# Grouping the small attention matmuls of three units into one TensorE step (attention followed by a gated MLP)

## The chip, the cores and the metric

The kernel runs on one core of a Trainium2 chip. The metric is the device time of one execution in microseconds (us). TensorE (PE) does the matrix products, PEld is its weight load, DVE is VectorE, ACT is ScalarE, POOL is GpSimd, and SP issues the DMAs. The engines run side by side and wait for each other through semaphores; each executes its own instructions strictly in program order.

## The reference

There are 4 batches, 8 heads, 768 tokens and 64 features per head. Attention has a local part (keys within 16 tokens) and a summary part (24 blocks of 32 tokens, whose key is the block's maximum and whose value is the block's mean).

```
k_sum = k.reshape(B, H, nb, block, D).max(axis=3)
v_sum = v.reshape(B, H, nb, block, D).mean(axis=3)
scores_l = scale * (q @ k^T), kept where |i - j| < 16
scores_s = scale * (q @ k_sum^T) + log(32)
a = softmax over both parts
x = a @ concat(v, v_sum)                     # 768 x 512 per batch
xk = mu_k * x + (1 - mu_k) * x_prev          # x_prev: one token earlier
xr = mu_r * x + (1 - mu_r) * x_prev
out = sigmoid(xr @ w_r) * (relu(xk @ w_k)**2 @ w_v)
```

All data is float32. The products of the second part are each done as three products of 32-bit "r" values (high times high, high times low, low times high).

## The kernel before, in words

Attention is cut into *units*: one unit is one batch, one pair of heads and one half of the tokens, so there are 8 units to a batch and 32 in all. A unit goes through these steps.

- Scores on PE (line 501): 12 products, each on a 64x64 part of the array, float32, which show as 24 instructions in the trace, into two PSUM tiles `sc`.
- Mask and row minimum on DVE (512), exponential and row sum on ACT (516), six of each; then the sum's epsilon on ACT (521) and its reciprocal `rc` on DVE (523).
- Normalisation of the six slices by `rc`, the *norms*: on POOL or DVE (528) or on ACT (533), whichever the planner expects to be done first.
- Two *turns* on PE (540): three transposes each, into the only PSUM tile `pt`, each copied to `pts` by ACT (544).
- Values on PE (562): 12 products, 24 instructions, into the only PSUM tile `av`, copied out to `x` by DVE (574) or ACT (576).

A value window holds 96 token rows and 24 rows of block means. For batch 0 the means come from small products (437, 457) and are spread by POOL or DVE (465). For batches 1 to 3, `load_set` loads the values of one head pair transposed into a staging tile `st` (448, SP), sums blocks on DVE (449), transposes the 24 sums on PE (452), scales them on ACT (471) and writes them into the windows by DMA (474). So this happens 12 times.

The second part of the work is *wide* on PE: every product uses 128 rows and 128 columns of the array. A gate step is 12 products of 512 columns (639 to 641); the first expert layer has steps of 12 products of 384 columns (671); the second has steps of 6 and 3 products of 512 columns (693, 719). There are two halves of 384 tokens per batch, each with a gate, eight first-layer and eight second-layer steps. Weights are loaded as 64-bit words and converted at the start (343 to 382) on ACT, POOL and DVE.

The order on each engine is made at build time by a list scheduler, `Plan.schedule`. It takes operations by a start time, a due time (worked backward from gates and experts) and the constants in `LENGTH`; `NUDGE` shifts the due times of named tags. One `op` on PE is one step: its products stay together. Attention of batch b+1 is planned in between the experts of batch b, so that PE takes attention steps between wide steps. Until the first gate is done, idle time that the plan foresees on PE is filled by products on a zero tile `still` (788).

Of the kernel before, what the change touches and what calls it, by code (L numbers as in the profile page):

```python
# [39 lines left out]
    score=865, transpose=370, vtrans=200, vpool=900, vsel=240, spread=560, spread_p=900, values=1000, values0=1750, mixe=1480, minus=200, diag=290, wminus=1250, wevac=520, none=0, gate=2790, gate_p=2100, e1=2110,  # L40
    e2a=1400, e2b=700, e2=700, e2h=350, resulth=340,
    kred=860, kred2=460, kmax=90, kcopy=225, vred=865, mask=203, rc=110, evac=470, mixd=530, sub=472, psub=480, khv=300,
    result=605, wsign=575, eps=110, wor=605, wsub=605, tiny=60, wsign_d=335,
    exp=378, pts=362, vm=165, mixa=512, cast=405, relu=375, square=413, sigmoid=494, wscale=562, wcast=510,
    norm=340, norm_d=165, norm_a=285, mixa_d=300, wscale_p=575, wcast_p=575, mixa_p=575, kcopy_p=400, evac_a=362,
# [11 lines left out]
APART = False  # L57
# [5 lines left out]
    e000=-16000, e001=-1500, e002=-500, e003=2000, e004=1500, e005=1500, e006=-11000, e007=12500, e010=7500,  # L63
    e012=2500, e014=-59000, e015=-2500, e016=-4000, e017=50000, e100=-12000, e101=-5500, e102=-52000,
    e103=-1500, e106=7000, e107=34000, e111=-1000, e112=-9500, e113=-2500, e114=-41500, e115=4500, e116=2000,
    e117=2500, e200=17500, e201=-35500, e202=1500, e203=15500, e204=49000, e205=57000, e206=60000, e207=59500,
    e210=1500, e211=-11500, e212=6500, e213=26500, e214=28000, e215=27000, e216=42000, e217=58000, e300=1500,
    e301=500, e302=-38500, e303=-4000, e304=13000, e305=14000, e306=12000, e307=58500, e310=-42500, e311=-25000,
    e313=2000, e314=2000, e316=17500, e317=50500, f000=60000, f001=1500, f002=14000, f003=4000, f004=-26000,
    f005=-31500, f006=3500, f007=-27000, f011=-3000, f014=-15500, f015=13500, f016=-11500, f017=-500,  # L70
    f100=-1500, f101=-6500, f102=19000, f104=5500, f105=-4000, f106=36000, f107=-22500, f111=-12000, f113=-6500,
    f115=-14500, f116=16000, f117=-2000, f201=-500, f202=2000, f203=23000, f204=-39000, f206=-22000,
    f207=-21000, f210=-13000, f211=10500, f212=1000, f213=20500, f214=-54500, f215=-56500, f217=1500,
    f300=-30000, f301=-19500, f302=-25000, f303=1000, f304=57000, f305=22500, f307=23000, f310=-4500,
    f311=-57500, f314=10500, f315=-17000, f316=500, gate00=8500, gate01=43000, gate10=5500, gate11=-16000,
    gate20=38500, gate21=59500, gate30=-4000, gate31=59500, mix000=-3000, mix001=-1500, mix010=-11000,
    mix011=500, mix101=-23500, mix111=7000, mix200=-500, mix201=-9500, mix210=16000, mix211=3500, mix300=-28000,
    mix301=-23500, mix310=-15000, mix311=26000, set00=1000, set01=13000, set02=-7500, set10=-11000, set11=-5500,
    set12=-500, set13=-9500, set20=1000, set21=-16000, set23=1500, set30=4000, set31=-17500, set32=-6500,
    set33=13500, unit000=1500, unit011=500, unit020=500, unit021=-1000, unit030=-2500, unit031=3000,  # L80
    unit100=-60000, unit101=-6000, unit110=-6000, unit111=-7500, unit120=-41000, unit130=500, unit131=7500,
    unit200=1000, unit201=-1500, unit210=-1000, unit211=6000, unit221=8500, unit300=1000, unit301=-42000,
    unit310=-500, unit311=1000, unit320=-13500, unit321=7000, unit330=-38500, unit331=-60000, wk1=8000,
    wk3=-5000, wk4=2000, wk5=-9500, wk6=-7000, wk7=-45000, wr0=500, wr1=-1000, wr2=-3000, wr3=2000, wv0=2000,
    wv1=6500, wv2=4500, wv3=-56500, wv4=-33500, wv5=500, wv7=-5500,
# [9 lines left out]
NORM = "DVE", "ACT"  # L95
# [161 lines left out]
def tile_kernel(ctx: ExitStack, tc: tile.TileContext, q, k, vT, v, mask, ident, pool, sel, mu, w_k, w_v, w_r, out):  # L257
# [4 lines left out]
    def tiles(name, n, shape, dtype=F32, pool=const):  # L262
# [5 lines left out]
        vs=tiles("vs", 1, [P, NS]), vm=tiles("vm", 4, [P, P]), sp=tiles("sp", 2, [P, P]),  # L268
# [120 lines left out]
    def windows(vw):  # L389
        return vw.t[0:NK, 0:S].rearrange("p (w d) -> p w d", d=P)  # L390

    def load_set(b, p):
# [17 lines left out]
        kg, ks, vm = buf("kg"), buf("ks"), buf("vm")  # L410
# [19 lines left out]
        if b == 0:  # L430
            tp = buf("mm")

            def means():
                for i in range(3):
                    for g in range(4):
                        w = 3 * g + i
                        nc.tensor.matmul(
                            tp.t[32 * g:32 * g + 32, 0:P], pool_sb[:, 4 - 2 * i:36 - 2 * i],
                            windows(vw[w // HW])[:, w % HW, :], start=(i == 0), stop=(i == 2))

            op("PE", "vpool", None, means, reads=[(x, y) for x in vw for y in "ab"] + [*POOLM], writes=[(tp, 0)])
        else:
            vt, vs, tp = buf("st"), buf("vs"), buf("pt")

            def tokens():
                return vt.t[:, 0:S].bitcast(F32)

            op("SP", "load", None, lambda: nc.sync.dma_start(out=tokens(), in_=vT[b - 1, p]), writes=[(vt, 0)], size=P * S * 4)
            op("DVE", "vred", None, lambda: nc.vector.tensor_reduce(
                out=vs.t, in_=tokens().rearrange("p (n c) -> p n c", c=BLOCK), op=ALU.add, axis=AX.X),  # L450
               reads=[(vt, 0)], writes=[(vs, 0)])
            op("PE", "vtrans", None, lambda: nc.tensor.transpose(
                out=tp.t[0:NS, 0:P], in_=vs.t, identity=ident_sb), reads=[(vs, 0), *IDENT], writes=[(tp, 0)])
        if b == 0:
            sp, t2 = buf("sp"), buf("mm")
# [5 lines left out]
            if APART:  # L461
                e["vm"] = vm
            for x in () if APART else vw:
# [6 lines left out]
        else:  # L470
            op("ACT", "vm", None, lambda: nc.scalar.activation(
                vm.t[0:NS], tp.t[0:NS, 0:P], AF.Copy, scale=1.0 / BLOCK), reads=[(tp, 0)], writes=[(vm, 0)])
            for x in vw:
                op("SP", "load", None, lambda x=x: nc.sync.dma_start(
                    out=windows(x)[QW:KB], in_=vm.t[0:NS].unsqueeze(1).broadcast_to([NS, HW, P])),
                   reads=[(vm, 0)], writes=[(x, "b")], size=NS * HW * 512)
        return e

    def unit(b, p, hf, e, due):

        plan.tag = f"unit{b}{p}{hf}"
        kt, qt, vw = e["kt"], buf("qt"), e["vw"][hf]
        o = hf * HW
        op("SP", "load", None, lambda: nc.sync.dma_start(out=qt.t, in_=q[b, p, :, hf * HT:(hf + 1) * HT]),
           writes=[(qt, 0)], size=P * HT * 4)
        sc = [buf("sc") for _ in range(2)]
        y = [buf("y") for _ in range(2)]
        mn = [buf("mn") for _ in range(2)]
        sm, rc = buf("sm"), buf("rc")
        pt = [buf("pt") for _ in range(2)]  # L490
        pts = [buf("pts") for _ in range(2)]
        av = buf("av")


        def scores():
            for i in range(NSL):
                for h in range(2):
                    for c in range(2):
                        n = 2 * i + c
                        hs, cs, w = slice(h * D, (h + 1) * D), slice(c * QW, (c + 1) * QW), o + n  # L500
                        nc.tensor.matmul(  # L501
                            sc[h].t[cs, i, 0:NK], qt.t[hs, n * QW:(n + 1) * QW], kt.t[hs, w * KB:w * KB + NK],
# [3 lines left out]
        op("PE", "score", due - 10000, scores, reads=[*e["kparts"], (kt, "s"), (qt, 0)],  # L506
           writes=[(sc[0], 0), (sc[1], 0)])
        for h in range(2):
            for i in range(NSL):
                slot = hf * NSL + i  # L510
                var = 0 if slot == 0 else (2 if slot == 2 * NSL - 1 else 1)
                op("DVE", "mask", None, lambda h=h, i=i, var=var: nc.vector.tensor_tensor_reduce(  # L512
                    out=y[h].t[:, i, :], in0=sc[h].t[:, i, 0:NK], in1=mask_sb[:, var, :], scale=-SCALE, scalar=3.0e38,
                    op0=ALU.add, op1=ALU.min, accum_out=mn[h].t[:, i:i + 1]),
                   reads=[(sc[h], 0), *MASK], writes=[(y[h], i), (mn[h], i)])
                op("ACT", "exp", None, lambda h=h, i=i: nc.scalar.activation(  # L516
                    y[h].t[:, i, :], y[h].t[:, i, :], AF.Exp, bias=mn[h].t[:, i:i + 1], scale=-1.0,
                    accum_out=sm.t[:, NSL * h + i:NSL * h + i + 1]),
                   reads=[(y[h], i), (mn[h], i)], writes=[(y[h], i), (sm, NSL * h + i)])

        op("ACT", "eps", None, lambda: nc.scalar.activation(sm.t, sm.t, AF.Copy, bias=1.0e-9),
# [360 lines left out]
```

## Time and profile before

| what | value |
|---|---|
| median of 3 runs | 458.22 us (457.29 to 458.62) |
| profiled execution | 457.95 us |
| its span, first to last instruction | 456.1 us |
| PE busy | 448.0 us (98%) |
| DVE busy | 298.5 us (65%) |
| ACT busy | 296.2 us (65%) |
| POOL busy | 25.2 us (6%) |
| DMA queue of the loads and stores | 33.4% of 16 engines |

The time is the profiled execution's own time; about 1.85 us of it lie outside the span. Busy time of PE is modelled from pipelined matmuls, so a busy PE may still hide short waits. In the chain of waits each piece is the time that a stretch of work adds to the end: end of the piece before it to its own end.

### The profile page before, as it was taken

The page shows a single profiled execution, that of the slowest core. Times are in us where ns is not written, and L with a number is a line of the kernel's source. Part 1 is how long each engine was busy: PE and PEld are TensorE (multiplying, and loading weights), DVE is VectorE, ACT ScalarE, POOL GpSimd, SP SyncE. Part 2 cuts the span into 40 slices and gives each one's busy share as a digit, 9 for nine tenths or more (in the row PEclk, how much of TensorE's full clock was granted, in tenths as well). Part 3 has the DMA queues.
Part 4 walks back from the last instruction along what each step waited for, and adds up shares of the span by engine and source line. Part 5 has one row for each costly group of instructions (what it writes and reads, how often), then busy time and mean ns, then how long its engine had stood idle before and what let it go on. Part 6 is the DMA issues. An engine that isn't in the chain of part 4 may idle for free.

```text
span 456.1 us, 9735 instructions
## 1 busy us (share of the span) xinstructions
PE 448.0 (98%) x3599; PEld 378.2 (83%) x3599; DVE 298.5 (65%) x1016; ACT 296.2 (65%) x879; POOL 25.2 (6%) x54
## 2 busy tenths in 40 slices
PE   9999999999999999999999999999999999999996
PEld 8766788788988898888978897888888889889985
DVE  5999999999773956647565547958552456243122
ACT  3898999889785837588576548857775546232210
POOL 0332310001000000000000000100000000000000
PEclk9999999999999999999999999999999999999999
DMA  8963558665100085252300058414300010001001
GB/s 306 401 238 128 204 196 279 235 205 191 32 15 15 1 268 226 47 170 82 126 15 9 6 189 311 100 49 138 133 17 13 1 46 24 0 2 68 2 0 69
DMA packets 27446, 51.96 MB, mean 114 GB/s; under 512 B 2951, under 2 KB 15111, under 8 KB 27399
## 3 DMA queue, kind: packets, MB, share of 16 engines
q1 hardware_dynamic: 27399, 51.35, 33.4%
q8 instruction: 28, 0.46, 0.4%
q14 instruction: 19, 0.16, 0.1%
HBM read 43.28 MB, written 6.29 MB: 109 GB/s over the span
## 4 chain that ended last, share of the span: by engine, by line
PE 78%; DVE 16%; DMA 2%; issue 1%; ACT 1%; SPq 1%; DVEq 0%
PE mm L671 27%; PE mm L693 24%; PE av L562 4%; PE mm L639 4%; PE mm L641 4%; PE mm L640 4%; PE pt L540 4%; PE sc L501 4%; PE mm L719 4%; DVE y L528 2%; DVE we L355 2%; DVE wc L359 2%; DVE y L512 2%; DMA qt<-in_q 1%; DVE we L351 1%
## 5 line engine op out<-in xcount | busy, mean ns | idle before, releaser
L671 PE MATMUL mm<-xs,wk_h 128*128 128x384 f32 x512 | 101.6, 340 | 0.0
L671 PEld LDWEIGHTS mm<-xs,wk_h 128*128 128x128 f32 x512 | 89.9, 188 | 4.5 <-issue 0.5
L516 ACT ACTIVATE y<-y,mn 128x120 f32<-128x120 f32 x192 | 73.8, 387 | 9.2 <-DVE mn L512 8.9
L676 ACT ACTIVATE r<-mm 128x384 f32<-128x384 f32 x64 | 30.7, 488 | 73.3 <-PE mm L671 56.7
L693 PE MATMUL mm<-wv_h,kh 128*128 128x512 f32 x168 | 69.0, 411 | 0.0
L693 PE MATMUL mm<-wv_l,kh 128*128 128x512 f32 x168 | 66.4, 395 | 0.0
L512 DVE CUSTOM_DVE_ANT_0 y<-sc,mask_sb 128x120 f32<-128x120 f32 x192 | 43.2, 276 | 20.9 <-PE sc L501 11.7
L671 PE MATMUL mm<-xs,wk_l 128*128 128x384 f32 x256 | 55.2, 337 | 0.0
L682 DVE TENSOR_TENSOR kl<-r,kh 128x384 fp32r<-128x384 f32 x64 | 35.2, 553 | 28.5 <-PE mm L693 27.6
L680 DVE CAST kh<-r 128x384 fp32r<-128x384 f32 x49 | 17.3, 358 | 55.3 <-ACT r L678 27.4
L693 PE MATMUL mm<-wv_h,kl 128*128 128x512 f32 x168 | 51.4, 414 | 0.0
L671 PEld LDWEIGHTS mm<-xs,wk_l 128*128 128x128 f32 x256 | 45.6, 188 | 0.0
L599 DVE TENSOR_TENSOR xs<-xa,xs 128x384 fp32r<-128x384 f32 x60 | 32.5, 548 | 18.7 <-ACT xs L597 18.6
L639 PE MATMUL mm<-wr_h,xs 128*128 128x512 f32 x96 | 38.7, 404 | 0.0
L641 PE MATMUL mm<-wr_h,xs 128*128 128x512 f32 x96 | 38.0, 396 | 0.0
L640 PE MATMUL mm<-wr_l,xs 128*128 128x512 f32 x96 | 37.9, 395 | 0.0
L693 PEld LDWEIGHTS mm<-wv_h,kh 128*128 128x128 f32 x168 | 31.6, 188 | 7.0 <-issue 0.8
L544 ACT COPY pts<-pt 120x384 f32<-120x384 f32 x64 | 30.3, 474 | 10.3 <-PE pt L540 8.0
L693 PEld LDWEIGHTS mm<-wv_l,kh 128*128 128x128 f32 x168 | 31.7, 188 | 5.9
L516 ACT ACTIVATION_READ_ACCUMULATOR y<-y,mn 128x1 f32 x192 | 36.3, 189 | 0.0
L594 DVE SCALAR_TENSOR_TENSOR xa<-vx,mu_sb,xa 128x384 f32<-128x384 f32 x60 | 35.8, 611 | 0.5 <-ACT xa L587 0.2
L540 PE MATMUL pt<-ident_sb,y 128*120 128x128 f32 x192 | 32.7, 278 | 1.5 <-ACT pts L544 1.2
(82 smaller groups left out, 694.3 us busy)
## 6 DMA issues: line engine op xcount, KB each, us to landing
vx<-in_v SPq DMA_DIRECT2D x32, 384.0 KB
kt<-in_k SPq DMA_DIRECT2D x15, 544.0 KB
qt<-in_q SPq DMA_DIRECT2D x32, 192.0 KB
out<-z SPq DMA_DIRECT2D x23, 256.0 KB
st<-in_vT SPq DMA_DIRECT2D x12, 384.0 KB
st<-in_w_k SPq DMA_DIRECT2D x8, 512.0 KB
st<-in_w_v SPq DMA_DIRECT2D x8, 512.0 KB
st<-in_w_r SPq DMA_DIRECT2D x4, 512.0 KB
```

What stands on the lines that cost most here:

```text
L512: op("DVE", "mask", None, lambda h=h, i=i, var=var: nc.vector.tensor_tensor_reduce(out=y[h].t[:, i, :], in0=sc[h].t[:, i, 0:NK], in1=mask_ ...
L516: op("ACT", "exp", None, lambda h=h, i=i: nc.scalar.activation(y[h].t[:, i, :], y[h].t[:, i, :], AF.Exp, bias=mn[h].t[:, i:i + 1], scale=-1.0,
L540: nc.tensor.transpose(out=pt[h].t[0:NK, i * P:(i + 1) * P], in_=y[h].t[:, i, :], identity=ident_sb)
L594: op("DVE", "mixd", None, lambda xt=xt, xa=xa, p=p: nc.vector.scalar_tensor_tensor(out=xa.t, in0=xt.t[:, 1 + lo:1 + lo + HT], scalar=mu_sb ...
L599: op("DVE", "sub", None, lambda xa=xa, xh=xh, xl=xl: nc.vector.tensor_tensor(out=xl.t, in0=xa.t, in1=xh.t.bitcast(F32), op=ALU.subtract), ...
L639: nc.tensor.matmul(ps[i].t, xh.t[:, ts], wr_h[:, p, :], start=(p == 0), stop=False)
L640: nc.tensor.matmul(ps[i].t, xh.t[:, ts], wr_l[:, p, :], start=False, stop=False)
L641: nc.tensor.matmul(ps[i].t, xl.t[:, ts], wr_h[:, p, :], start=False, stop=(p == NPAIR - 1))
L671: nc.tensor.matmul(ps.t[:, 0:HT], w[:, j, p, :], x[p][s].t, start=(n == 0), stop=(n == 11))
L676: op("ACT", "relu", None, lambda: nc.scalar.activation(r.t, ps.t[:, 0:HT], AF.Relu), reads=[(ps, 0)], writes=[(r, 0)])
L682: op("DVE", "sub", None, lambda: nc.vector.tensor_tensor(out=kl.t, in0=r.t, in1=kh.t.bitcast(F32), op=ALU.subtract), reads=[(r, 0), (kh, 0 ...
L693: nc.tensor.matmul(acc[t].t, a.t[:, t * P:(t + 1) * P], w[:, j, :], start=start, stop=stop)
```

## The change

- The unit becomes a class `Unit`, whose `scores`, `turn` and `values` return what they would emit. `group` puts several of them into one PE step.
- From batch 1 on, `chain(b)` walks the 8 units. Its step i holds, in this order, the scores of unit i, the values of unit i-2 and the first turn of unit i-1. The second turn of unit i-1 stays a step of its own. A batch has one step with scores alone, one with scores and a turn, six with all three, one with values and a turn, and one with values alone.
- `block_means(b)` loads the transposed values of all four head pairs, sums their blocks into one 128x96 tile, and turns it in one transpose, with one scaled copy. So there are 3 such transposes and copies instead of 12; loads, DVE sums and the DMAs into the windows remain.
- `NORM` loses DVE: norms go to POOL or ACT.
- Constants in `LENGTH` and the whole `NUDGE` table are other numbers. `APART`, which was off, goes.

```diff
-NORM = "DVE", "ACT"
+NORM = ('ACT',)
...
-        vs=tiles("vs", 1, [P, NS]), vm=tiles("vm", 4, [P, P]), sp=tiles("sp", 2, [P, P]),
+        vs=tiles("vs", 1, [P, NPAIR * NS]), vm=tiles("vm", 4, [P, P]), sp=tiles("sp", 2, [P, P]),
...
+    def block_means(b):
+        plan.tag = f"means{b}"
+        vs, tp, vm = buf("vs"), buf("pt"), buf("vm")
+        for p in range(NPAIR):
+            vt = buf("st")
...
+            op("SP", "load", None, lambda p=p, tokens=tokens: nc.sync.dma_start(out=tokens(), in_=vT[b - 1, p]),
+               writes=[(vt, 0)], size=P * S * 4)
+            op("DVE", "vred", None, lambda p=p, tokens=tokens: nc.vector.tensor_reduce(
+                out=vs.t[:, NS * p:NS * p + NS], in_=tokens().rearrange("p (n c) -> p n c", c=BLOCK), op=ALU.add, axis=AX.X),
+               reads=[(vt, 0)], writes=[(vs, p)])
+        op("PE", "vtrans", None, lambda: nc.tensor.transpose(
+            out=tp.t[0:NPAIR * NS, 0:P], in_=vs.t, identity=ident_sb),
+           reads=[(vs, p) for p in range(NPAIR)] + [*IDENT], writes=[(tp, 0)])
+        op("ACT", "vm", None, lambda: nc.scalar.activation(
+            vm.t[0:NPAIR * NS], tp.t[0:NPAIR * NS, 0:P], AF.Copy, scale=1.0 / BLOCK), reads=[(tp, 0)], writes=[(vm, 0)])
+        return vm
...
+    def group(name, due, *parts):
+        emits = [x for x, _, _ in parts]
+        op("PE", name, due, lambda: [x() for x in emits],
+           reads=[r for _, rs, _ in parts for r in rs], writes=[w for _, _, ws in parts for w in ws])
...
+    def chain(b):
+
+        means = block_means(b)
+        units, n = [], 2 * NPAIR
+        for i in range(n + 2):
...
+            if i < n:
+                parts.append(units[i].scores())
+                due.append(units[i].due - 10000)
+            if i >= 2:
+                parts.append(units[i - 2].values())
+                due.append(units[i - 2].due - 1000)
+            if 1 <= i <= n:
+                parts.append(units[i - 1].turn(0))
+                due.append(units[i - 1].due - 3500)
...
-            for p in range(NPAIR):
-                e = load_set(b + 1, p)
-                for h in range(2):
-                    unit(b + 1, p, h, e, gate_due(b + 1, 0) - 14000 - (7 - 2 * p - h) * UNITS)
+            chain(b + 1)
```

PE, in the middle of batch 1's attention, before: the end of one unit's values (`av`), the transpose of one head pair's block sums (`vs_82`), a wide step (`wv`), a turn (`pt<-ident_sb,y`) and another wide step.

```order
L562 MATMUL av_146<-pts_104,vx_73 64x64
L452 MATMUL pt_145<-ident_sb,vs_82 24x128
L693 MATMUL mm_147<-wv_h,kh_133 128x512
L693 MATMUL mm_147<-wv_l,kh_133 128x512
L693 MATMUL mm_148<-wv_h,kh_133 128x512
L693 MATMUL mm_148<-wv_l,kh_133 128x512
L693 MATMUL mm_150<-wv_h,kh_133 128x512
L693 MATMUL mm_150<-wv_l,kh_133 128x512
L540 MATMUL pt_145<-ident_sb,y_89 120x128 x3
L693 MATMUL mm_147<-wv_h,kl_135 128x512
L693 MATMUL mm_148<-wv_h,kl_135 128x512
L693 MATMUL mm_150<-wv_h,kl_135 128x512
```

PE, the first full chain step of batch 1, after: the end of its scores and the start of its values.

```order
L511 MATMUL sc_143<-kt_62,qt_66 64x120 x2
L511 MATMUL sc_144<-kt_62,qt_66 64x120 x2
L577 MATMUL av_146<-pts_103,vx_72 64x64
L577 MATMUL av_146<-pts_104,vx_72 64x64
...
L557 MATMUL pt_145<-ident_sb,y_91 120x128 x3
L703 MATMUL mm_150<-wr_h,xs_114 128x512
L704 MATMUL mm_150<-wr_l,xs_114 128x512
```

Scores (`sc`), all twelve products of the values (`av`) and a turn now stand without a wide product between them; the wide gate products (`wr`) follow the turn. In the old order wide products stood between the values and the turn.

DVE, during batch 0's attention, before: norms (`y<-y,rc`) of two units between the pieces of weight conversion (`we`, `wc`).

```order
L523 RECIPROCAL rc_102<-sm_99 128x6
L528 TENSOR_SCALAR y_89<-y_89,rc_102 128x120 x3
L528 TENSOR_SCALAR y_90<-y_90,rc_102 128x120 x3
L355 SCALAR_TENSOR_TENSOR we_139<-st_137,we_139 128x512
L523 RECIPROCAL rc_100<-sm_97 128x6
L359 SCALAR_TENSOR_TENSOR wc_141<-wc_141,we_139 128x512
L528 TENSOR_SCALAR y_91<-y_91,rc_100 128x120 x2
L528 TENSOR_SCALAR y_92<-y_92,rc_100 128x120 x3
L465 COPY vx_74<-vm_86 24x768
```

DVE at the like place, after, with the reciprocal that belongs to the fourth unit.

```order
L385 TENSOR_TENSOR wk_l<-wc_141,wk_h 128x512
L535 RECIPROCAL rc_100<-sm_97 128x6
L686 TENSOR_TENSOR xs_117<-mm_148,xs_116 128x384
L475 COPY vx_74<-vm_86 24x768
L475 COPY vx_75<-vm_86 24x768
L475 COPY vx_72<-vm_85 24x768
L358 SCALAR_TENSOR_TENSOR we_139<-st_136,we_139 128x512
L358 SCALAR_TENSOR_TENSOR we_140<-st_138,we_140 128x512
L362 SCALAR_TENSOR_TENSOR wc_141<-wc_141,we_139 128x512
L362 SCALAR_TENSOR_TENSOR wc_142<-wc_142,we_140 128x512
```

No norm stands on DVE any more; copies that spread batch 0's means (`vx<-vm`) and weight pieces follow the reciprocal instead.

More of the change, by code (lines that the diff above doesn't have):

```diff
@@ L68 @@
[L68 to L77, printed above, removed]
@@ L501, in scores @@
                         nc.tensor.matmul(
-                            sc[h].t[cs, i, 0:NK], qt.t[hs, n * QW:(n + 1) * QW], kt.t[hs, w * KB:w * KB + NK],
+                            av.t[hs, w * QW:(w + 1) * QW], windows(vw)[:, w, hs], pts[h].t[:, i, c * QW:(c + 1) * QW],
                             start=True, stop=True,
                         )
-        op("PE", "score", due - 10000, scores, reads=[*e["kparts"], (kt, "s"), (qt, 0)],
-           writes=[(sc[0], 0), (sc[1], 0)])
-        for h in range(2):
[L509 to L519, printed above, removed]
@@ L567, in unit @@
[L567 to L576 removed]
+            return emit, [(vw, x) for x in "ab"] + [(pts[0], 0), (pts[1], 0)], [(av, 0)]
@@ new lines, in group, with unit @@
+    def group(name, due, *parts):
+        emits = [x for x, _, _ in parts]
+        op("PE", name, due, lambda: [x() for x in emits],
+           reads=[r for _, rs, _ in parts for r in rs], writes=[w for _, _, ws in parts for w in ws])
+    def unit(*args):
+        u = Unit(*args)
+        group("score", u.due - 10000, u.scores())
+        u.soften()
+        for h in range(2):
+            group("transpose", u.due - 3500 + 800 * h, u.turn(h))
+            u.copy(h)
+        group("values", u.due - 1000, u.values())
+        u.keep()
@@ new lines, in chain @@
+    def chain(b):
[3 more added lines that the diff above has]
+            if i < n:
+                p, hf = divmod(i, 2)
+                if not hf:
+                    e = load_set(b, p, means)
+                units.append(Unit(b, p, hf, e, gate_due(b, 0) - 14000 - (n - 1 - i) * UNITS))
+            plan.tag = f"chain{b}{i}"
+            parts, due = [], []
+            if i < n:
+                parts.append(units[i].scores())
[6 more added lines that the diff above has]
+                due.append(units[i - 1].due - 3500)
+            group({1: "score", 2: "scoreT", 3: "chain"}[len(parts)] if i < n else {1: "values", 2: "valuesT"}[len(parts)], min(due), *parts)
+            if i >= 2:
+                units[i - 2].keep()
+            if 1 <= i <= n:
+                u = units[i - 1]
+                u.copy(0)
+                group("transpose", u.due - 2700, u.turn(1))
+                u.copy(1)
+            if i < n:
+                units[i].soften()
```

228 lines of the change are left out of this document (124 added, 104 removed).

## The prediction

> **What bounds the kernel now.** I read the page first, then the busy time by stage, then the chain of waits.
>
> The page's first rows, and the busy time in six stretches (start:end, length, then busy us of PE, PEld, DVE, ACT, POOL with instruction counts, granted clock, DMA share, GB/s):
>
> ```profile
> span 456.1 us, 9735 instructions
> PE   9999999999999999999999999999999999999996
> 10.00:28.00 18.00, 17.11 (x266) 13.45 (x262) 16.97 (x71) 14.98 (x60) 6.12 (x12) 1.00 1.03 389
> 28.00:56.00 28.00, 25.99 (x295) 18.69 (x296) 27.87 (x103) 25.42 (x90) 8.20 (x12) 1.00 0.46 155
> 56.00:110.00 54.00, 53.59 (x422) 44.02 (x421) 54.00 (x158) 49.83 (x136) 5.11 (x10) 1.00 0.69 226
> 110.00:370.00 260.00, 260.00 (x2166) 220.24 (x2166) 166.71 (x619) 179.13 (x544) 5.40 (x17) 1.00 0.27 89
> ```
>
> From 110 to 370 us PE is busy for all 260 us at full clock, while DVE and ACT have about a third of their time free. There the time is the sum of what PE executes, and nothing else. Before 56 us it is different: PE idles 2.0 us of 28, and DVE has 0.13 us left. So two things must be priced: the PE order of the whole program, and DVE, ACT and POOL in the first 110 us (the head).
>
> The chain of waits of a stretch in the middle gives what each kind of PE piece adds to the end (start, us, line and count):
>
> ```profile
> 99.86 0.33 PE pt L540 x3
> 100.19 0.70 PE mm L693 x3
> 100.89 0.78 PE sc L501 x24
> 101.67 0.85 PE av L562 x24
> ...
> 111.53 2.09 PE mm L671 x12
> 113.61 0.85 PE av L562 x24
> 114.46 0.78 PE sc L501 x24
> 115.24 0.21 PE pt L452
> 115.45 2.12 PE mm L671 x12
> ...
> 123.30 0.47 PE pt L540 x3
> 123.77 1.40 PE mm L693 x6
> ...
> 125.50 0.78 PE sc L501 x24
> 126.27 0.90 PE mm L693 x3
> ...
> 139.17 0.11 PE pt L452
> ...
> 147.45 1.60 PE mm L693 x6
> ```
>
> Scores cost 0.78 and values 0.85 whatever stands before them, values right behind scores included (101.67). The price of a small step is paid by what follows it. A wide step of three products takes 0.70 behind a turn and 0.90 right behind scores; one of six takes 1.40 behind a turn and 1.60 behind values: 0.20 in both. A turn takes 0.33 behind wide work and 0.47 behind values: 0.14, and the wide step after it pays nothing. A transpose of block sums takes 0.11 behind wide work and 0.21 behind scores.
>
> **The change on PE.** I counted, over the whole order of before and after, what follows scores and values. Wide work directly: 34 times before, 9 after. A turn: 15 before, 29 after. A transpose of block sums: 5 before, 1 after. Block-sum transposes in all: 12 and 3. The number of scores, values, turns, gate and expert products is the same.
>
> - Direct exits: 25 fewer at 0.20 = -5.0 us.
> - Exits through a turn: 14 more at 0.14 = +2.0 us.
> - Block-sum transposes: 9 fewer at 0.11 = -1.0 us, and 4 fewer that also pay 0.10 = -0.4 us.
> - First-layer steps now stand behind a second-layer step 43 times instead of 37; the rows show 2.12 against 2.09, so 6 x 0.03 = +0.2 us.
>
> The sum is -4.2 us. All of it is on the path in the stretch where PE never idles.
>
> Rows that the next steps use (busy us, mean ns, then idle time of the engine before):
>
> ```profile
> L449 DVE TENSOR_REDUCE vs<-st 128x24 f32<-128x768 f32 x12 | 11.3, 945 | 1.7 <-PE pt L452 1.7
> L533 ACT ACTIVATE y<-y,rc 128x120 f32<-128x120 f32 x48 | 17.0, 389 | 5.2 <-DVE rc L523 5.2
> L528 POOL TENSOR_SCALAR y<-y,rc 128x120 f32<-128x120 f32 x6 | 2.6, 445 | 33.0 <-DVE rc L523 33.0
> L465 DVE COPY vx<-vm 24x768 f32<-24x768 f32 x2 | 1.8, 883 | 0.1
> L788 PE MATMUL av<-still 128*128 128x128 f32 x104 | 15.9, 316 | 1.0 <-POOL still L782 1.0
> L471 ACT ACTIVATE vm<-pt 24x128 f32<-24x128 f32 x12 | 3.0, 253 | 0.5 <-PE pt L452 0.5
> L355 DVE SCALAR_TENSOR_TENSOR we<-st,we 128x512 uint32<-128x512 uint32 x20 | 13.5, 681 | 0.0
> L351 DVE TENSOR_SCALAR we<-st 128x512 f32<-128x512 f32 x17 | 7.7, 470 | 5.2 <-DMA st<-in_w_r 5.0
> L512 DVE CUSTOM_DVE_ANT_0 y<-sc,mask_sb 128x120 f32<-128x120 f32 x192 | 43.2, 276 | 20.9 <-PE sc L501 11.7 <-PE pt L540 9.0
> ```
>
> What could hide behind it: a chain step is one piece on PE, so if the turn's norms are late, PE stands, and the wide steps queued behind it stand too, then their relu on ACT and the accumulation after it. The nearest row is the unit at 145.82: its scores end at 146.60 and its first turn runs at 151.82 with no gap before it, so 5.2 us are enough for mask, exponential and norm.
>
> ```profile
> 145.82 0.78 PE sc L501 x24
> ...
> 151.82 0.33 PE pt L540 x3
> ...
> 136.56 0.97 ACT L533 ACTIVATE y<-y,rc 128x120 f32<-128x120 f32 x3
> ```
>
> Adding up the piece prices above along the new order, the shortest such distance in batches 1 to 3 is 7.4 us. Norms on ACT come every 0.29 us ((0.97 - 0.39)/2, with the mean of ACT's row above), so six of them end 1.7 us after their first start; if all of that came on top of the 5.2 us, 6.9 is still below 7.4. I take nothing for it; without that cover, each 0.1 us by which norms are late costs 24 x 0.1 = 2.4 us over the 24 chain steps with a turn.
>
> Block means: all four loads of a batch use three `st` tiles, so the fourth waits on SP for the first DVE sum, and the loads and mean DMAs behind it wait too. The sum takes 0.95 us (first of these rows). In the new order the first values of batch 1 stand some 10 us of PE work behind the block transpose, which hides it. The nine ACT copies that go are 2.3 us of an engine with 81 us free in the middle: nothing.
>
> **The change in the head.** The 138 norms of DVE go: by the order ACT has 111 instead of 48 and POOL 81 instead of 6. The chain of waits of the first 62 us, by line, and four pieces of DVE and POOL:
>
> ```profile
> by line: DVE y L528 15.5%; DVE y L512 10.8%; DMA qt<-in_q 9.3%; DVE we L355 8.6%; DMA mu_sb<-in_mu 6.9%; DVE kg L413 5.6%; issue 5.4%; DVE wc L359 4.3%; ACT y L516 3.8%; DVE xs L599 3.1%; DVE we L351 2.9%; DVE vx L465 2.8%; DVE xs L622 2.7%
> ...
> 25.25 1.24 DVE L528 TENSOR_SCALAR y<-y,rc 128x120 f32<-128x120 f32 x6
> ...
> 34.18 2.05 DVE L528 TENSOR_SCALAR y<-y,rc 128x120 f32<-128x120 f32 x5
> 34.34 0.67 POOL L351 TENSOR_SCALAR we<-st 128x512 f32<-128x512 f32 x1 [2.25 <-ACT vm L459]
> 35.07 0.88 POOL L465 COPY vx<-vm 24x768 f32<-24x768 f32 x1
> ```
>
> Here DVE is the chain: its norms alone are 15.5% of 62 us, 9.6 us. Up to the first expert step, DVE now has 30 norms less and four more spreads (4 x 0.88 = 3.5 us), five more 0.68 us pieces of weight conversion and two of 0.47 (4.3 us) and 6 masks less (6 x 0.28 = -1.7 us): -9.6 + 6.1 = -3.5 us. That is the bound below. The other bound: the new order has six more fillers on the zero tile (58, not 52); two instructions of 0.15 us each (15.9/104) make +1.8 us if they stand in PE's way. ACT gets 1.4 us more in the same stretch and had 2.6 us free from 28 to 56. I take -0.7 us, near the middle, since neither row is nearer.
>
> The Trainium skill (SBUF — State Buffer, section "Who interferes with whom") says that GpSimd and VectorE share a port pair which one of them holds for a whole instruction while the other is fully blocked. That speaks against 75 more norms on POOL. The trace agrees that something like it exists: five DVE norms took 2.05 us beside two POOL instructions, six took 1.24 us without one. Only 12 of the POOL norms lie ahead of the first expert step, 12 x 0.445 = 5.3 us, and four POOL spreads of 0.88 us leave, so POOL's share there grows by 2 us, inside the bounds above.
>
> Sum: 457.95 - 4.2 - 0.7 = 453.05 us for an execution like the profiled one, which is 0.27 us below the median of the runs; so **453.3 us**. Its own range is 452.0 to 455.8: half way to the lower bound, which is a rival's, and all the way to the upper.
>
> **The rivals.**
>
> *DVE was the bound of the head, and frees it entirely.* The whole -3.5 us come, and of the 2.0 us that PE idled from 28 to 56 nothing is left to fillers. For it speaks DVE's 27.87 of 28 us. Against it: ACT is at 25.42 of 28 and gets more. Time: 457.95 - 4.2 - 3.5 + 0.3 = 450.5 us. Chance 0.22.
>
> *The grouping saves less, since values behind scores pay for their weights.* The Trainium skill (TensorE: Matmul & The Clock Gate, section "The mechanism" of Part 3) says that a weight load overlaps running matmuls only when it goes to other row groups. The values load 120 rows, which all score tiles use. As a mechanism here: each of the 18 full chain steps pays 0.20 us at the change from scores to values, as wide work does. That is +3.6 us: 457.95 - 0.7 - 4.2 + 3.6 = 456.7, with the 0.27 456.9: no measurable change (I call 0.3%, 1.4 us, what a measurement of this kernel can tell). By that rule the row at 101.67 should be longer than the one at 113.61; the trace disagrees, both are 0.85. Chance 0.08.
>
> *ACT becomes the bound of the head.* Place: 56 to 110 us, where ACT is at 49.83 of 54. Up to the last cast that the second half's experts need, the order gives ACT 29 more norms and 2 more exponentials, and 3 weight casts, 2 mixes, 1 sigmoid and 1 cast fewer. At 0.29 us a norm that is 29 x 0.29 + 0.8 - 3.6 = 5.6 us; at 0.389 it is 8.4 us. ACT's 4.2 us of idle can take part of it. If none fits, because ACT idles only when its inputs are missing, the casts come 5.6 to 8.4 us later and PE has nothing else: 457.95 - 4.2 + 7.0 = 460.8, slower. It decides from 5.6 us on (4.2 and the 1.4). Against it: the new order runs the last two units of batch 0 later, so ACT has first-layer work to take in the meantime. Chance 0.08.
>
> **How the numbers follow.** The first case has 0.62, the others 0.22, 0.08 and 0.08. Faster by over 0.3%: the first two and a trace of the ACT case, 0.85. Within 0.3%: the weight-load case and part of the ACT case, 0.09. Slower: 0.06. The range from 450.3 to 456.5 holds the first two cases with some margin for the bounds, and leaves out about 0.16.
>
> The first expert step of before, in the order of time:
>
> ```profile
> 54.64 1.65 PE L671 MATMUL mm<-xs,wk_h 128*128 128x384 f32 x8
> ```
>
> **What would show it.** Right: PE busy without a gap from 110 to 370 still; turns at 0.47 behind values; some 9 wide steps left with the extra 0.20; block transposes 3; DVE without norms; the first expert step between 51 and 57 us (before: 54.64). Wrong: rows of PE waiting for norms in front of chain steps; values longer than 0.85 behind scores; ACT full and PE waiting for its casts or copies before 110 us; the head longer by more than 2 us.

## The result, and the profile after

The changed kernel takes 455.29 us (median of 20 runs, 454.15 to 458.07), the kernel before, measured beside it, 457.66 us (20 runs, 457.04 to 459.15). The ratio is 0.995, with a 95% interval from 0.9939 to 0.9961: faster by 2.4 us, which is inside the range forecast, but about half of the 4.4 us that the forecast of 453.3 us put on those 457.66. The profiled execution took 454.91 us against 457.95 us before, 3.0 us less. Here and below, medians are over the executions in the faster of the chip's two states, which leaves out one of the 12 of a_nofill and one of the 6 of a_norm0.

The first rows of the page after the change, and the busy time in the same stretches as before (start:end, length, then PE, PEld, DVE, ACT, POOL with counts, granted clock, DMA share, GB/s):

```profile
span 453.1 us, 9740 instructions
PE   9998999999999999999999999999999999999996
```

```profile
10.00:28.00 18.00, 17.71 (x267) 14.20 (x258) 16.76 (x66) 14.98 (x63) 9.56 (x16) 1.00 1.04 389
28.00:56.00 28.00, 25.67 (x284) 19.05 (x283) 27.42 (x79) 26.60 (x92) 9.70 (x16) 1.00 0.52 178
56.00:110.00 54.00, 52.88 (x420) 43.50 (x420) 52.22 (x155) 51.66 (x152) 10.80 (x21) 1.00 0.69 221
110.00:370.00 260.00, 260.00 (x2173) 223.46 (x2172) 145.96 (x514) 182.89 (x566) 28.61 (x80) 1.00 0.27 90
```

PE still has no gap from 110 to 370 us. In the two stretches ahead of that it is busy for 0.32 and 0.71 us less than before, although the first of them now holds 1.81 us of fillers, where there were none; from 10 to 28 us it is busy for 0.60 us more.

The chain of waits in the middle of batch 1 (start, us, line and count; 511 is scores, 577 values, 557 a turn, 735 and 757 the expert layers):

```profile
128.15 0.78 PE sc L511 x24
128.93 0.85 PE av L577 x24
129.78 0.47 PE pt L557 x3
130.25 2.08 PE mm L735 x12
132.34 0.33 PE pt L557 x3
...
178.60 0.11 PE pt L409
...
180.12 0.78 PE sc L511 x24
180.89 0.90 PE mm L757 x3
```

One grouped step reads 0.78, 0.85, 0.47: the same three prices as before, and the wide step behind it (2.08) pays nothing. The row at 180.89 is one of the 9 wide steps that still stand right behind scores or values; counted over both traces there are 34 of them before and 9 after, and 15 and 29 turns there. These are the numbers of the forecast.

The chain of the first 62 us by line, the wait that PE has there, and the pieces around it:

```profile
by line: PE av L849 19.9%; ACT y L529 11.1%; ACT y L545 9.3%; PE sc L511 7.6%; PE mm L680 7.3%; PE mm L735 6.6%; PE mm L461 3.8%; ACT pts L564 3.5%; ACT xs L661 2.8%; ACT vx L593 2.6%; DVE we L354 2.5%; issue 2.3%; PE pt L557 2.2%; ACT L719
```

```profile
PE mm L680 <- ACT y L529: 1.7, 1, 1.7
```

```profile
43.94 0.58 ACT y L545 x2
44.52 0.36 ACT vx L593
44.89 1.15 ACT y L529 x6
...
46.07 1.54 PE mm L680 x4
```

Before, VectorE's norms led this list with 15.5%. Now it is fillers (849), and ScalarE's exponentials (529) and norms (545). At 46.07 the products with the diagonals wait for ScalarE, 1.7 us; ahead of them on that engine stand two norms, then the copy of the values (593), then exponentials. The first expert step begins at 54.15 us:

```profile
54.15 1.66 PE L735 MATMUL mm<-xs,wk_h 128*128 128x384 f32 x8
```

Three marks of each trace tell the parts of the program apart: the first expert step, the first expert step of the second half of batch 0, and the end of the last product on PE. The stretch between the last two is called *the middle* below.

| kernel | first expert step | second half's first | PE's end | middle |
|---|---|---|---|---|
| before | 54.64 | 108.85 | 452.33 | 343.48 |
| after | 54.15 | 109.14 | 449.30 | 340.16 |

The new order has one step of scores (0.78 us) fewer ahead of the first mark and one more in the middle; it also has one turn (0.33 us) more between the two marks and one fewer in the middle. So on equal work the middle became 3.32 + 0.78 - 0.33 = 3.8 us shorter, and what lies ahead of it 0.29 + 0.78 - 0.33 = 0.7 us longer. The sum, -3.0 us, is what PE's end moved (452.33 to 449.30).

### The profile page after: what moved, and what is told of

Read it like the earlier page. It is cut to its first block, busy times and chain, and to the rows that moved or that the text cites. A ratio compares the mean times of both kernels' runs of the same rounds, so it can differ in the third digit from the quotient of the medians.

```text
span 453.1 us, 9740 instructions
## 1 busy us (share of the span) xinstructions
PE 444.6 (98%) x3602; PEld 379.4 (84%) x3602; DVE 273.4 (60%) x876; ACT 304.3 (67%) x923; POOL 59.2 (13%) x137
## 4 chain that ended last, share of the span: by engine, by line
PE 85%; ACT 6%; DVE 5%; issue 1%; DMA 1%; POOL 0%; DVEq 0%; POOLq 0%
PE mm L735 27%; PE mm L757 23%; PE av L577 5%; PE sc L511 5%; PE pt L557 5%; PE mm L703 4%; PE mm L704 4%; PE mm L705 4%; PE mm L783 3%; PE av L849 3%; ACT y L529 2%; ACT y L545 1%; DMA st<-in_w_k 1%; PE mm L680 1%; DVE wc L362 1%
## 5 line engine op out<-in xcount | busy, mean ns | idle before, releaser
L744 DVE CAST kh<-r 128x384 fp32r<-128x384 f32 x56 | 20.2, 361 | 62.5 <-PE mm L757 32.5
L540 POOL TENSOR_SCALAR y<-y,rc 128x120 f32<-128x120 f32 x81 | 30.7, 395 | 202.0 <-DVE rc L535 196.4
L757 PE MATMUL mm<-wv_h,kl 128*128 128x512 f32 x168 | 50.4, 409 | 0.0
L525 DVE CUSTOM_DVE_ANT_0 y<-sc,mask_sb 128x120 f32<-128x120 f32 x192 | 42.1, 277 | 7.4 <-PE sc L511 7.3
L663 DVE TENSOR_TENSOR xs<-xa,xs 128x384 fp32r<-128x384 f32 x60 | 32.2, 557 | 15.6 <-ACT xs L661 15.5
L545 ACT ACTIVATE y<-y,rc 128x120 f32<-128x120 f32 x111 | 35.8, 387 | 5.2 <-DVE rc L535 4.7
```

The lines of the kernel that those rows point to most:

```text
L545: nc.scalar.activation(y[h].t[:, i, :], y[h].t[:, i, :], AF.Copy, scale=rc.t[:, NSL * h + i:NSL * h + i + 1])
L663: op("DVE", "sub", None, lambda xa=xa, xh=xh, xl=xl: nc.vector.tensor_tensor(out=xl.t, in0=xa.t, in1=xh.t.bitcast(F32), op=ALU.subtract), ...
L757: nc.tensor.matmul(acc[t].t, a.t[:, t * P:(t + 1) * P], w[:, j, :], start=start, stop=stop)
```

## The experiments

The theory: the gain is the PE order alone, paid out in the middle, at 0.20 us for each change from small products straight to wide ones; what was hoped for ahead of the middle did not come, since work taken from VectorE's list came back to it or landed on ScalarE. The rivals are those of the prediction, and that the new numbers in the tables, not the grouping, made the gain. Ratios and their intervals are those on record, to the kernel before on the same chip (457.89 to 458.07 us there); they are not quotients of the medians.

| run | median, us | ratio (95%) | first expert step | second half's first | middle |
|---|---|---|---|---|---|
| a_same | 455.89 | 0.9941 (0.9919 to 0.9962) | 53.20 | 109.62 | 340.74 |
| a_split | 461.00 | 1.0064 (1.0046 to 1.0082) | 54.93 | 111.94 | 344.80 |
| a_swap | 459.92 | 1.0029 (1.0008 to 1.0051) | 54.83 | 110.72 | 343.51 |
| a_vt | 459.45 | 1.0025 (1.0007 to 1.0044) | 54.85 | 111.75 | 342.17 |
| a_nofill | 457.15 | 0.9974 (0.9954 to 0.9994) | 56.57 | 111.07 | 340.37 |
| a_norm0 | 461.36 | 1.0073 (1.0046 to 1.0101) | 59.63 | 114.66 | 340.27 |
| a_pool24 | 457.26 | 0.9984 (0.9971 to 0.9997) | 54.16 | 110.81 | 340.25 |
| a_pool12 | 455.71 | 0.9956 (0.9938 to 0.9974) | 54.31 | 109.42 | 340.19 |
| a_spread0 | 456.13 | 0.9965 (0.9946 to 0.9983) | 52.94 | 108.76 | 340.18 |
| b_sums | 455.27 | 0.9928 (0.9909 to 0.9947) | 54.21 | 108.95 | 340.35 |
| b_normmid | 458.83 | 1.0004 (0.9988 to 1.0020) | 54.64 | 111.79 | 340.58 |
| b_signmid | 456.15 | 0.9962 (0.9942 to 0.9982) | 53.43 | 109.26 | 341.25 |

**a_same: the changed kernel as it is**, once more.

> The changed kernel unaltered, as the mark for the others of this set. All theories: the time of the changed kernel again, 455.3 us, 0.995 of the kernel before.

455.89 us, 0.9941: the gain comes again. Its first mark came 0.95 us earlier than in the profile after, and its second mark 0.48 us later; the middle differs by 0.58 us. Single traces say less than that suggests. Eight traces (after, a_same, a_split, a_swap, a_vt, b_sums, b_normmid, b_signmid) run the same lists up to the first mark, and it lies between 53.20 and 54.93 us; ten run the same list in the middle (all but a_split, a_swap and a_vt, and before), and it lasts from 340.16 to 341.25 us.

**a_split: the grouping undone, all else kept.** Between the parts of each of the 24 grouped steps that are followed by wide work, one wide product of the following step is run.

```diff
-            o.emit()
+            if o in inside:
+                o.parts[0]()
+                hooks.extend(o.parts[1:])
+            else:
+                o.emit()
...
+    def wide(*args, **kw):
+        nc.tensor.matmul(*args, **kw)
+        if hooks:
+            hooks.pop(0)()
```

> All 24 grouped steps with two or three parts get one wide product of the step that follows put between each two of their parts; everything else keeps its place. Theory (the time in the middle is the sum of PE's pieces, and each exit from scores or values into wide work costs 0.20 us, each exit into a turn 0.14): a step of three then pays 0.20 + 0.20 in place of 0.14, so 18 x 0.26 + 6 x 0.06 = +5.0 us, about 460.3 us and slower than before. Rival (the gain came from the retuned order of the rest, not from the grouping): no change, 455.3 us. Rival (values behind scores pay for their weights anyway): 18 x 0.20 less, +1.4 us.

The chain of waits of this run (286 is the wide product):

```profile
184.37 0.78 PE sc L517 x24
185.15 7.17 PE mm L286 x36
192.32 0.78 PE sc L517 x24
193.10 0.43 PE mm L286
193.53 0.33 PE pt L563 x3
```

461.00 us, 5.1 us above a_same, where 5.0 were expected; 4.1 of them lie in the middle, where its own counts give 4.7. The single wide product at 193.10 adds 0.43 us; the five that follow the turn behind it take 1.17 us, 0.23 each. With the same lists and tables the gain is gone, and the kernel is slower than before. So the new numbers without the grouping do not make the gain, and the 0.20 us fit as a price: this order has 51 wide steps right behind scores or values and 5 turns there, against 9 and 29, and 42 x 0.20 - 24 x 0.14 = 5.0. That also settles the rival by which values pay for their weights behind scores: undoing the groups would then have cost less.

**a_swap: the turn ahead of the values** in each grouped step.

```diff
-            if i >= 2:
-                parts.append(units[i - 2].values())
-                due.append(units[i - 2].due - 1000)
             if 1 <= i <= n:
                 parts.append(units[i - 1].turn(0))
                 due.append(units[i - 1].due - 3500)
+            if i >= 2:
+                parts.append(units[i - 2].values())
+                due.append(units[i - 2].due - 1000)
```

> The turn stands before the values in each grouped step instead of behind them; nothing else moves. Theory (what is paid depends on what stands last): the turn still pays 0.14 behind the scores, and the values' exit into wide work now pays 0.20, so 18 x 0.20 + 3 x 0.06 = +3.8 us, 459.1 us. Rival (a group is paid once, in whatever order): no change, 455.3 us.

The chain of this run:

```profile
197.82 0.78 PE sc L511 x24
198.60 0.47 PE pt L557 x3
199.07 0.85 PE av L577 x24
199.92 0.43 PE mm L757
```

459.92 us, 4.0 us above a_same, with 3.8 expected; 2.8 of the 4.0 lie in the middle by the traces, where the counts give 3.6, and the rest lies ahead of it, where the traces of one list differ by more than that. The turn costs 0.47 behind scores as it does behind values, and now the values leave into wide work (the first product at 199.92 takes 0.43, as in a_split). So the order within the group matters as much as the group: the turn has to come last, since it is what makes the exit cheap.

**a_vt: nine more transposes of block sums.** Each of the three is repeated behind the next three wide steps, into an unused part of the `av` tile.

```diff
-    end, early = 600, True
+    end, early, again = 600, True, 0
...
+        if o.name == "vtrans":
+            again, source = 3, o.bufs[0].t
+        elif o.eng == "PE" and again and o.name in ("gate", "e1", "e2a"):
+            again -= 1
+            nc.tensor.transpose(out=spare[0:NPAIR * NS, 0:P], in_=source, identity=ident_sb)
```

> Each of the three transposes of block means is run three more times, each extra one behind one of the next three wide steps, into a part of a tile that nobody reads. Theory (0.11 us for each behind wide work, 0.10 to 0.14 more in none): 9 x 0.11 = +1.0 us, 456.3 us. Rival (a transpose hides beside wide work or costs its full 0.28 us): 0 or +2.5 us.

459.45 us, 3.6 us above a_same: a miss. The waits of this run from 56 to 114 us, of ScalarE and of PE (line 856 is the repeated transpose):

```profile
ACT vx L593 <- PE av L856: 4.0, 2, 2.4
```

```profile
PE mm L735 <- ACT xs L661: 1.0, 1, 1.0
```

The repeated transposes write into the tile that holds the values. ScalarE's copy of the values had to wait for them, 4.0 us in two waits; its later work came late, and PE waited 1.0 us for its cast right behind the second mark. So this run measured a wait that the experiment itself made. The middle is 0.9 to 2.0 us longer than in the ten traces with the unaltered list; without that 1.0 us, at most 1.0 us is left for the six transposes there, 0.17 us each, which does not speak against 0.11 and does not show it either.

**a_nofill: without the 32 fillers after the first 26.**

```diff
-            for _ in range(int((o.start - end) // WARM)):
+            for _ in range(int((o.start - end) // WARM) if end == 600 else 0):
```

> The 32 fillers behind the first 26 are left out; they compute nothing that is used. Theory (fillers stand in time in which PE waits for ACT, DVE or a load anyway): within 0.5 us of 455.3. Rival (the six more fillers of the changed order stand in PE's way, 0.25 to 0.3 us each): 1 to 2 us faster, 453.8 us. Rival (they keep the granted clock up): the clock falls below 1.00 between 10 and 36 us and the time grows by 2 us or more.

Two stretches of 6 us of this run, and the first of them in the changed kernel:

```profile
20.00:26.00 6.00, 4.70 (x35) 2.94 (x33) 5.66 (x14) 4.42 (x17) 3.38 (x7) 0.50 1.05 390
26.00:32.00 6.00, 6.00 (x81) 4.25 (x80) 4.94 (x27) 5.77 (x23) 3.28 (x6) 0.81 0.70 227
```

```profile
20.00:26.00 6.00, 5.71 (x90) 4.18 (x87) 5.91 (x25) 5.20 (x19) 4.93 (x10) 1.00 1.05 384
```

457.15 us, 1.3 us above a_same, and the first expert step 2.4 us later than in the profile after. Without fillers the granted clock falls to 0.50, and returns while PE is busy again. The Trainium skill (TensorE: Matmul & The Clock Gate, section "What's actually happening" of Part 1) says that the clock is halved after a window of some 3.4 us in which PE was idle and full again after a busy one. The 0.50 agrees, and so does the rise once PE is busy for all 6.00 us. That PE has to be idle for a whole such window does not show here: its longest idle time ahead of the fall was 2.34 us (10.06 to 12.40 us, with two shorter ones behind it). So leaving most of the fillers out gains nothing. What the six additional ones alone cost, as my upper bound had it, is not separated from the clock here. Whether leaving fillers out costs something is less sure: the second mark is 1.5 to 1.9 us later than in after and a_same, but the intervals of the two ratios overlap. That fillers (849) lead the list of the chain in the head does not mean that they delay it.

**a_norm0: the 24 norms of ScalarE ahead of the first expert step on VectorE.**

```diff
+    moved = [o for o in order[:first] if o.name == "norm" and o.eng == "ACT"]
+    for o in moved:
+        o.emit = o.dve
```

> The 24 norms that ACT runs ahead of the first expert step are run by DVE at the same place of the list. Theory (ACT took over from DVE as the bound of the head: PE waits 1.7 us for ACT at 44 us): ACT loses 24 x 0.29 = 7 us up to the first expert step, and that step starts 1 to 2 us earlier, about 453.8 us. Rival (DVE is as full as ACT there, 27.4 of 28 us): DVE gains 24 x 0.19 = 4.6 us or more, the first expert step starts 2 to 4 us later, about 458 us.

```profile
28.00:56.00 28.00, 22.92 (x218) 16.14 (x219) 27.54 (x91) 18.14 (x70) 9.58 (x14) 0.94 0.46 148
```

461.36 us, 5.5 us above a_same, all of it ahead of the first expert step (59.63 us); the rival had said 2 to 4 us. VectorE stays full and ScalarE falls to 18.14 of 28 us. A part may be the clock: its mean of 0.94 in this stretch takes at most 1.7 us from PE. In the new list VectorE has other work where its norms were (spreads and weight conversions), and could not have kept them. So taking the norms off VectorE is worth some 5 us to this list, though it is worth nothing against the list before: what left the engine was replaced.

**a_pool24, a_pool12, a_spread0: ScalarE or VectorE relieved ahead of the first expert step.** The 24 norms of ScalarE, or every second one, go to GpSimd; or the six spreads of VectorE do.

```diff
+    moved = [o for o in order[:first] if o.name == "norm" and o.eng == "ACT"]   # pool12: [1::2]
+    for o in moved:
+        o.emit = o.pool
...
+    spreads = [o for o in order if hasattr(o, "pool") and o.name.startswith("spread") and o.eng == "DVE"]   # spread0
+    for o in spreads:
+        o.emit = o.pool
```

> The kernel after the change, with the 24 norms that ScalarE runs ahead of the first expert step run by GpSimd instead, at the same places of the list. Theory: after the change ScalarE sets the pace of the head together with VectorE (26.60 and 27.42 of 28 us from 28 to 56 us, and the multiplication with the diagonals waits 1.7 us for a copy that stands behind norms and exponentials on ScalarE). 24 x 0.29 = 7.0 us leave ScalarE and 24 x 0.395 = 9.5 us go to GpSimd, which has 9.70 of 28 us busy. If ScalarE's norms are what holds the head, the first expert step comes 1 to 3 us earlier than in the unaltered kernel (53.20 and 54.15 us in its two profiles), and the time is about 453.3 us, 0.990 of before. Rival 1: VectorE, which keeps all its work, holds the head anyway: first expert step between 53 and 55 us, 0.995. Rival 2: the norms now stand behind weight conversions in GpSimd's list, and the turns on TensorE wait for them: first expert step 2 us later or more, 1.000 or above.

> The same with every second of these 24 norms: 12 x 0.29 = 3.5 us leave ScalarE, 12 x 0.395 = 4.7 us go to GpSimd. Theory (ScalarE's norms hold the head): first expert step 0.5 to 1.5 us earlier than in the unaltered kernel, about 0.992 of before. Rival 1 (VectorE holds it): 0.995. Rival 2 (GpSimd's queue): half of what the run with 24 loses.

> The kernel after the change, with the 6 spreads of batch 0's block means that VectorE runs put on GpSimd at the same places of the list (before the change 4 of the 8 were on VectorE's side of this list and 4 on GpSimd's; after it 6 and 2). 6 x 0.88 = 5.3 us leave VectorE. Theory (VectorE is as full as ScalarE in the head, each holds it for a part): first expert step 1 to 2 us earlier than in the unaltered kernel, about 0.992 of before. Rival 1 (ScalarE alone holds it): no change, 0.995. Rival 2: the spreads stand behind weight conversions on GpSimd, and the values, which read what they write, wait: first expert step 1 to 3 us later, 0.998 or above.

The stretch from 28 to 56 us, of a_pool24 and of a_spread0:

```profile
28.00:56.00 28.00, 26.56 (x285) 19.36 (x284) 27.02 (x79) 22.62 (x76) 24.45 (x32) 1.00 0.50 170
```

```profile
28.00:56.00 28.00, 26.11 (x285) 19.40 (x285) 26.96 (x74) 27.08 (x93) 15.34 (x19) 1.00 0.54 187
```

None is measurably faster than the changed kernel. In a_pool24 ScalarE is at 22.62 of 28 us and the first expert step is at 54.16 us all the same, but GpSimd is at 24.45 there, PE waits 0.8 us for its norms up to the second mark, and the time is 1.4 us above a_same. So this run alone could hide a gain behind GpSimd. With half of the norms moved (a_pool12) PE has no such wait, and still nothing changes that can be measured (first expert step at 54.31 us): ScalarE's norms do not hold it, and my theory of a bound on ScalarE fell. With the spreads moved the first expert step comes at 52.94 us, 0.3 us ahead of the earliest of the eight traces with an unaltered list up to there (53.20 to 54.93 us), and the second mark at 108.76; the time shows nothing of it. (Before the change VectorE had two of the eight spreads and GpSimd six, by the rows of their copies, not four and four.)

**b_sums, b_normmid, b_signmid: the stretch between the two marks.** The four block sums of batch 1 over 4 of 32 tokens; or ScalarE's 19 norms there on GpSimd; or VectorE's 7 signs and 3 mixes there on GpSimd.

```diff
-                in_=tokens().rearrange("p (n c) -> p n c", c=BLOCK), op=ALU.add, axis=AX.X),
+                in_=tokens().rearrange("p (n c) -> p n c", c=BLOCK)[:, :, 0:BLOCK if b > 1 else 4], op=ALU.add, axis=AX.X),
...
+    moved = [o for o in order[first[0]:first[8]] if o.name == "norm" and o.eng == "ACT"]   # normmid
+    moved = [o for o in order[first[0]:first[8]] if o.name in ("wsign", "mixa") and o.eng == "DVE"]   # signmid
+    for o in moved:
+        o.emit = o.pool
```

> The kernel after the change, with the four block sums of batch 1 taken over 4 of each block's 32 tokens instead of all (that part of the computation is left out); the loads, the transpose and all waits stay. Theory: since one transpose turns a whole batch, all four sums of batch 1 (4 x 0.94 us) have to run on VectorE before the first values of that batch, in the stretch from 54 to 109 us, where before the change 2 of them ran; the chain of waits there leads over them and over what stands behind them on VectorE. With some 3 us less on VectorE, the second half's first expert step comes 0.8 to 1.5 us earlier than 109.14 and 109.62 us (the unaltered kernel), and the time is about 0.992 of before. Rival: the weight conversions and their loads set the pace there, and nothing moves: 109 to 110 us, 0.995.

> The kernel after the change, with the 19 norms that ScalarE runs between the first expert step and the second half's first one run by GpSimd, at the same places of the list: 19 x 0.29 = 5.5 us leave ScalarE (51.66 of 54 us busy), 19 x 0.395 = 7.5 us go to GpSimd (10.80 of 54). Theory that ScalarE, which took VectorE's norms, holds this stretch: the second half's first expert step comes 1 to 2 us earlier than 109.14 and 109.62 us, about 0.992 of before. Rival: VectorE holds it (its block sums and weight conversions), and relieving ScalarE brings nothing, as it brought nothing ahead of the first expert step: 109 to 110 us, 0.995.

> The kernel after the change, with 7 signs of the weights and 3 mixes that VectorE runs between the first expert step and the second half's first one run by GpSimd, at the same places of the list: 7 x 0.478 + 3 x 0.411 = 4.6 us leave VectorE (52.22 of 54 us busy) and some 10 us go to GpSimd, at the 1.00 us that a sign takes there. Theory that VectorE holds this stretch: the second half's first expert step comes 0.8 to 1.5 us earlier than 109.14 and 109.62 us, about 0.992 of before. Rival 1: the loads or ScalarE hold it: no change, 0.995. Rival 2: the signs are the first step of a weight's conversion and come later on the slower engine: 1 to 3 us later, 0.998 or above.

The chain of the changed kernel, and of b_sums at the same place:

```profile
90.09 1.72 DVE vs L406 x2
91.81 0.42 DVE xs L663
...
94.98 0.52 ACT xs L661
95.49 0.39 ACT pts L564
...
95.92 0.54 PE pt L557 x3
```

```profile
93.90 0.78 PE sc L511 x24
94.67 0.47 PE pt L557 x3
95.15 0.70 PE mm L757 x3
```

With the sums made short, the way over VectorE's sums and ScalarE's cast to the turn at 95.92 is gone, and the chain stays on PE there. In a_same PE waits for the sums directly:

```profile
PE pt L409 <- DVE vs L406: 0.7, 1, 0.7
```

So the four sums of batch 1 do hold PE up at this place, by 0.25 us ahead of the turn at 95.92 and by 0.7 us in a_same. What this is worth to the whole is not shown: in b_sums the second mark is at 108.95 us, 0.2 to 0.7 us earlier, where 0.8 to 1.5 were expected, and the interval of 0.9928 overlaps that of a_same.

The waits of PE in b_normmid from 54 to 112 us:

```profile
PE pt L558 <- ACT pts L565: 2.2, 2, 1.7
PE pt L558 <- POOL y L540: 0.9, 2, 0.6
```

b_normmid lost 2.9 us to a_same: the norms came late from GpSimd and the turns waited for them and for the copies behind them. So it tells nothing of whether ScalarE holds this stretch. b_signmid (0.9962) changed nothing that can be measured.

## Why the prediction was right, and where it was not

- **The PE order, -4.2 us: the prices were right; the place of 0.8 us of it was not.** The counts (34 to 9, 15 to 29, 12 to 3) and prices (0.20, 0.14, 0.11) are those of the trace, and undoing the group or turning it round gave back 5.1 and 4.0 us where the same prices said 5.0 and 3.8. But "all of it is on the path in the stretch where PE never idles" does not hold. Behind the second mark the counts are 24 to 5 exits into wide work, 10 to 22 into a turn, 11 to 2 block transposes (5 to 0 of them behind small products) and 33 to 39 first-layer steps behind second-layer ones: -3.8 + 1.7 - 1.0 - 0.5 + 0.2 = -3.4 us. The other -0.8 us lie ahead of it, where PE also waits for other engines. The middle measured -3.8 us on equal work, and -2.7 with the longest of its ten traces: -3.4 lies inside. The -1.5 us of the block transposes in this sum were not tested by themselves, since a_vt did not show their price.
- **Norms hidden in front of the turns: right.** Nothing waits from 110 to 370 us (260.00 of 260.00).
- **Values behind scores: right.** 0.85 in the group, and a_split refutes that rival by its size.
- **75 more norms on GpSimd: no cost seen.** VectorE's masks from 54 to 109 us took 275 ns each, before 272 (rows below). Other work on GpSimd does show: the subtraction of the weights' high part took VectorE 752 ns there, before 680 (L385, L382), which comes of two pieces of 1.01 and 1.15 us, each beside a weight conversion on GpSimd; none of them stands beside a norm there. Before, it was VectorE's norms that were lengthened so: up to the second mark 451 ns for the 18 beside a GpSimd instruction, 272 for the other 26.
- **ScalarE as the bound from 56 to 110 us, slower: did not come.** Of the 5.6 to 8.4 us nothing near that is seen; ScalarE went from 49.83 to 51.66 of 54 us. One of its signs was there ahead of that stretch, PE's wait of 1.7 us for ScalarE at 46.07 us; the runs that relieved ScalarE moved nothing by it.
- **VectorE freed entirely in the head, 450.5 us: did not come.**
- **The head, "I take -0.7 us, near the middle": this term was mis-sized.** With the -0.8 us of the PE order that lie there too, the forecast had -1.5 us ahead of the second mark. It measured +0.7 us on equal work, 2.2 us off. The bounds given for the term, -3.5 and +1.8, hold it. PE's busy time up to the second mark did not fall (104.56 us before, 104.41 after): fillers took 1.8 us more of it (15.89 and 17.72), and it stood idle for 4.29 and 4.73 us. Three things were wrong in how the term was made. First, the sum of VectorE's work ended at the first expert step; but that mark by itself is worth little: with first expert steps from 52.94 to 54.31 us (after, a_same, a_pool12, a_spread0, b_sums, b_signmid), the second mark is always between 108.76 and 109.62 us. (It is later in the runs that changed PE's order or fillers, gave VectorE norms, or gave GpSimd many.) The work up to the second mark had to be counted. Second, a spread on VectorE was priced at 0.88 us, the mean of one of 1.21 and one of 0.55 us; the six of the new order took 0.57 us each. That error by itself made the forecast gain too small, not too large. Third, VectorE did not become free from 54 to 109 us, although 14 norms left; these groups show a part of what moved (before, then after; busy us, mean ns):

```profile
L528 DVE TENSOR_SCALAR y<-y,rc 128x120 f32<-128x120 f32 x14 | 3.1, 270 | 0.0
L449 DVE TENSOR_REDUCE vs<-st 128x24 f32<-128x768 f32 x2 | 1.9, 938 | 0.0
L512 DVE CUSTOM_DVE_ANT_0 y<-sc,mask_sb 128x120 f32<-128x120 f32 x24 | 5.4, 272 | 0.0
L413 DVE TENSOR_REDUCE kg<-kt 128x48 f32<-128x768 f32 x3 | 2.8, 917 | 0.0
L382 DVE TENSOR_TENSOR wv_l<-wc,wv_h 128x512 fp32r<-128x512 f32 x7 | 4.8, 680 | 0.0
```

```profile
L406 DVE TENSOR_REDUCE vs<-st 128x24 f32<-128x768 f32 x4 | 3.7, 940 | 0.0
L525 DVE CUSTOM_DVE_ANT_0 y<-sc,mask_sb 128x120 f32<-128x120 f32 x30 | 6.6, 275 | 0.0
L437 DVE TENSOR_REDUCE kg<-kt 128x48 f32<-128x768 f32 x4 | 3.7, 936 | 0.0
L385 DVE TENSOR_TENSOR wv_l<-wc,wv_h 128x512 fp32r<-128x512 f32 x6 | 4.5, 752 | 0.0
```

Norms -3.1; block sums +1.8, masks +1.2, key maxima +0.9: +3.9. Weight conversion became less there, and in all VectorE's busy time from 56 to 110 us fell only from 54.00 to 52.22 us. One transpose for a whole batch needs all four sums ahead of it, where two had to be done here before. The prediction priced that pull at nothing, with "some 10 us of PE work" to hide it; PE waited 0.25 and 0.7 us for it in the two traces above.

- **What stays open.** No single engine was found whose relief moves the second mark by more than traces of one kernel differ. The 0.7 us rest on one trace before and one after, and traces of one list differ by more than that at the first mark; the medians (2.4 us gained, 3.8 in the middle by the traces) leave 1.4 us for the same part. Of that, the sums account for some tenths by PE's waits; the rest is not settled. One rival was tested by no run: the loads. In the chain of waits from 54 us to the second mark before the change, no load has a row; here one of weights stands in it, and in a_same one of transposed values as well:

```profile
69.23 4.78 DMA st<-in_w_k
```

```profile
86.95 4.36 DMA st<-in_vT
```

The batched step also issues its first load of transposed values at 81.6 us, where it was 91.3 us before.

No version here beats the changed kernel and keeps the whole computation.

## What to carry over

Where PE is the only bound, price the *changes* between kinds of product, not the products, and let the cheapest kind stand last in a group: here a turn behind scores and values pays 0.14 us once, where two exits into wide work pay 0.40. Where several engines are near full, a relief is counted up to the point where the streams meet again, not to the first milestone; and a batched step has to be charged for the inputs that it pulls forward.

## What the runs showed that I had not expected

Fillers do more than fill: without 32 of them the clock stood at 0.50 from 20 to 26 us with PE busy for 4.70 of 6 us, the first expert step came 2.4 us later, and nothing was gained. And a product that writes into an unused part of a tile is not free of that tile: ScalarE's copies waited 4.0 us for it.
